# Two bias additions merged into one VectorE operation that reads a shared PSUM product twice

## The chip, the cores and the metric

The kernel runs on one NeuronCore of a Trainium2 chip. The metric is the device time in microseconds of one execution, from launch to the last output byte; the time of a kernel is the median of its runs.

## What is computed

The input `x` is 8 batches of 3136 rows by 256 columns. The reference first mixes each batch in the frequency domain and then applies a gated feed-forward layer:

```python
X = np.fft.rfft(x, axis=1)
Yr = Xr @ w_r - Xi @ w_i + b_r
Yi = Xr @ w_i + Xi @ w_r + b_i
Y  = soft-threshold of (Yr, Yi) by 0.01          # shrink each part towards zero
y  = np.fft.irfft(Y, n=3136, axis=1)
h  = relu(y @ w_in)
g  = sigmoid(depthwise 3-tap convolution of h along the rows)
out = (h * g) @ w_out
```

The two bias vectors `b_r` and `b_i` have one entry per column. They are the data of the change.

## The kernel before, in words

The transform of length 3136 is done as 56 x 56, in two matmul stages each way, with scratch arrays in DRAM between them. The spectral part works in 56 items: 8 batches times 7 groups of 4 frequency columns. Every item passes through these steps, on an order written as one Python loop over `it` in which the steps of different items are interleaved (item `it` in stage 2, item `it-1` in `mix`, item `it-3` in stage 3, and two later pieces of stage 1):

- `stage1` (lines 240 to 248): one matmul of 512 columns per half piece into PSUM (L246), a copy by ScalarE (L247), a store to scratch.
- `stage2` (274 to 290): 16 short matmuls (L281) give the spectrum of an item. ScalarE copies one half to `d` (L284) and rounds the product to the high part `fh` (L285); VectorE makes `d` a difference (L286) and the low part `fl` (L287); then the same for `d` itself: `fh` by ScalarE (L288), `fl` by VectorE (L289). High and low parts exist because the matmuls run on rounded operands, three products for one.
- `mix` (292 to 323): 36 matmuls (L305) into three PSUM tiles `ps[0..2]` (printed as ps_mx), first `ps[2]`, the product that the real and the imaginary result have in common, then `ps[0]` and `ps[1]`. Each `ps[c]` is 128 partitions by 512 fp32 elements, one buffer each. VectorE adds `ps[2]` to the two halves of the bias tile, which gives `p1` (L310, twice; printed as p); adds `p1` to `ps[0]` and `ps[1]`, four additions on 64 partitions each, which gives `v` (L314); ScalarE makes `r = relu(v - 0.01)` (L319); VectorE makes the thresholded `v` (L320); ScalarE rounds it to `sh` (L321); GpSimd makes the rest `sl = v - sh` (L322). `p1`, `r` and `sl` have one buffer, `v` and `sh` two.
- `stage3` (325 to 335): 12 matmuls (L332) on `sh` and `sl`, a copy by ScalarE (L334), a store.

Beside the items, in iterations 3 to 55, a "background" generator converts the 64-bit weights `w_in` and `w_out` to two fp32 parts: eight pieces of 512 elements per partition, each some eleven VectorE operations (L185 to L192, L200, L201) and one ScalarE rounding (L199). Five steps of it are taken per iteration at first, later two or three.

The feed-forward part follows: `stage4` (L424 to L431), `up` (L433 to L459) and `down` (L464 to L485), driven by the loop from L502 on. It holds most of the matmuls (L443 and L471).

The order in which an engine meets its instructions is not the program order alone: a scheduler with a timeline model of its own sorts them per engine when the kernel is built, so a cheaper or dearer operation can move its neighbours. On the chip every engine then runs its list strictly in order. The semaphore waits follow from the tiles.

Of the kernel before, what the change touches and what calls it, by code (L numbers as in the profile page):

```python
# [13 lines left out]
ALU = mybir.AluOpType  # L14
# [3 lines left out]
B, S, D, FF = 8, 3136, 256, 1024  # L18
# [6 lines left out]
UG = 4  # L25
# [70 lines left out]
def spectral_ffn_kernel(ctx: ExitStack, tc: tile.TileContext, x, w_r, w_i, b_r, b_i,  # L96
                        w_in, conv_w, w_out, fwd1, fwd2, inv1, inv2, out):
    nc = tc.nc
    K1, K2 = 2 * R, 2 * SP
# [16 lines left out]
    with ExitStack() as ab:  # L116
# [15 lines left out]
        bias = cmx.tile([P, 2, UG // 2, D], F32, name="bias")  # L132
# [159 lines left out]
        def mix(xs):  # L292


            fh, fl = xs
            ps = [psm.tile([K2, UG // 2, D], F32, name=f"ps_mx{c}") for c in range(3)]
            for c in (2, 0, 1):
                q = (1, 2, 0)[c]
                for k in range(UG // 2):
                    mm = []  # L300
                    for t in range(NT):
                        a = [f[:, t, c, 2 * k:2 * k + 2, :] for f in (fh, fl)]
                        mm += [(a[0], wmix_hi[:, t, q, :]), (a[0], wmix_lo[:, t, q, :]), (a[1], wmix_hi[:, t, q, :])]
                    for n, (lt, rh) in enumerate(mm):
                        nc.tensor.matmul(ps[c][:, k, :], lt, rh, start=(n == 0), stop=(n == len(mm) - 1))  # L305
            p1 = wk.tile([K2, 2, UG // 2, D], F32, name="p1", bufs=1)
            v = wk.tile([K2, UG // 2, 2, D], F32, name="v")
            half = (slice(0, SP), slice(SP, K2))
            for c in range(2):
                nc.vector.tensor_tensor(p1[:, c], ps[2], bias[:, c], op=ALU.add)  # L310
            for c in range(2):
                for k in range(2):
                    src, dst = half[k], half[k if c == 0 else 1 - k]
                    nc.vector.tensor_tensor(v[dst, :, k, :], ps[c][src], p1[src, c], op=ALU.add)  # L314
            v = v.rearrange("p a b d -> p (a b) d")
            sh = wk.tile([K2, UG, D], F32R, name="sh")
            sl = wk.tile([K2, UG, D], F32R, name="sl", bufs=1)
            r = wk.tile([K2, UG, D], F32, name="r", bufs=1)
            nc.scalar.activation(r, v, AF.Relu, bias=mlam)  # L319
            thr = nc.vector.scalar_tensor_tensor(v, v, LAM, r, op0=ALU.add, op1=ALU.min)  # L320
            nc.scalar.copy(sh, v)  # L321
            SL_ENG.tensor_tensor(sl, v, sh.bitcast(F32), op=ALU.subtract)  # L322
            return sh, sl, thr
# [22 lines left out]
        p1 = NG  # L346
# [27 lines left out]
        for it in range(n_it + 3):  # L374
            if it + 2 < n_it:
                a2s[it + 2], _ = load_a2(*items[it + 2])
            if it < n_it:
                xs[it] = stage2(items[it][1], a2s.pop(it))
            if it < NG:
                load_inv1(it)  # L380
                if it + 1 < NG:
                    load_t2(it + 1)
            if 0 <= it - 1 < n_it:
                ss[it - 1] = mix(xs.pop(it - 1))
            if 0 <= it - 3 < n_it:
                stage3(*items[it - 3], ss.pop(it - 3))
            while p1 < n_it and p1 < min(it + AHEAD, NG + 2 + it + it // 2):
                stage1(*items[p1])
                p1 += 1
            if WP0 <= it < n_it:  # L390
                with tc.issue_after(ss[it - 1][2].ins):
                    for _ in range(5 if it < CW_IT else 2 + (it % 5 == 0)):
                        next(background, None)
# [148 lines left out]
```

## Time and profile before

| what | value |
|---|---|
| runs, us | 1767.83, 1800.61, 1798.17; median 1798.17 |
| profiled execution | span 1797.0 us; the page gives no other time for it |
| busy in the span | PE 97%, PE weight load 91%, DVE 87%, ACT 68%, POOL 8% |
| mean granted TensorE clock | 0.993 of full speed |
| spectral part | about 50 to 600 us |
| feed-forward part | about 600 to 1797 us |

The span runs from the first to the last instruction of the profiled execution; the median of the runs is 1.2 us above it. PE is TensorE's matmuls, PEld its weight loads, DVE VectorE, ACT ScalarE, POOL GpSimd. In a row of a timeline the first number is the start in us from the beginning of the span, the second the length; rows of equal operations that follow each other are merged with a count. Recorded lengths of neighbours on one engine overlap by a little, so the distance from one start to the next (the pitch) tells what an instruction really takes away from its engine. DVE "busy" also counts the time in which a started instruction is held up.

### The profile page before, as it was taken

What the parts mean: (1) busy time and instruction counts of PE and PEld (TensorE: products, weight loads), DVE (VectorE), ACT (ScalarE), POOL (GpSimd) and SP (SyncE); (2) the same over time, 40 slices, a digit from 0 to 9 for tenths busy, and PEclk for the clock granted to TensorE, in tenths of its full rate; (3) what the DMA queues carried; (4) which work ended last, traced back from release to release, by engine and by line L of the source; (5) the groups of instructions that cost most, each with busy time, mean ns of one, the idle gap of its engine ahead of it and who ended that gap; (6) DMA issues with size and microseconds to landing.
All of it is one profiled execution on the core that took longest, in us unless ns stands there. A gap on an engine that the chain in (4) does not pass through costs nothing.

```text
span 1797.0 us, 29407 instructions
## 1 busy us (share of the span) xinstructions
PE 1745.9 (97%) x12096; PEld 1627.7 (91%) x12096; DVE 1568.6 (87%) x1842; ACT 1223.6 (68%) x1579; POOL 134.9 (8%) x60
## 2 busy tenths in 40 slices
PE   6999999999999999999999999999999999999999
PEld 2788788888898899999999999999999999999998
DVE  2899999999998698888888898888888888888887
ACT  2666666666666677777677777767777777767766
POOL 0122222222223000000000000000000000000000
PEclk8999999999999999999999999999999999999999
DMA  9776676666562410011111001101101111100001
GB/s 257 224 244 207 177 213 191 186 201 202 164 168 72 132 52 21 22 52 52 32 52 52 32 32 52 52 32 52 52 26 58 52 42 42 42 22 21 21 22 42
DMA packets 107382, 164.63 MB, mean 92 GB/s; under 512 B 8816, under 2 KB 86000, under 8 KB 107248
## 3 DMA queue, kind: packets, MB, share of 16 engines
q1 hardware_dynamic: 107248, 162.74, 30.6%
q8 instruction: 96, 1.57, 0.4%
q14 instruction: 38, 0.31, 0.1%
HBM read 85.65 MB, written 77.07 MB: 91 GB/s over the span
## 4 chain that ended last, share of the span: by engine, by line
PE 70%; DVE 15%; issue 8%; DMA 3%; ACT 3%; SPq 0%; DVEq 0%; ACTq 0%
PE acc L471 31%; PE ps_h L443 31%; PE ps_s L424 5%; DVE v L314 5%; DVE fl L287 2%; PE ps_mx L305 2%; DMA i_raw<-in_inv_dram 2%; DVE p L310 2%; ACT r L319 2%; DVE fl L289 2%; DVE d L286 1%; DVE v L320 1%; PE ps_s L332 1%; PE ps_s L281 1%; DMA z<-sc 0%
## 5 line engine op out<-in xcount | busy, mean ns | idle before, releaser
L471 PE MATMUL acc<-wout,gh 128*128 128x256 f32 x3136 | 567.0, 280 | 0.0
L452 DVE SCALAR_TENSOR_TENSOR c<-h,cw,c 128x896 f32<-128x896 f32 x448 | 512.9, 1147 | 47.1 <-ACT c L450 46.1
L443 PE MATMUL ps_h<-yh,win 128*128 128x450 f32 x1792 | 550.8, 368 | 0.2
L471 PEld LDWEIGHTS acc<-wout,gh 128*128 128x128 f32 x3136 | 493.7, 188 | 6.5
L471 PE MATMUL acc<-wout,gl 128*128 128x256 f32 x1568 | 437.6, 281 | 0.0
L445 ACT ACTIVATE h<-ps_h 128x900 f32<-128x900 f32 x224 | 207.7, 927 | 254.6 <-PE ps_h L443 254.6
L443 PEld LDWEIGHTS ps_h<-yh,win 128*128 128x128 f32 x1792 | 338.7, 189 | 26.3 <-DVE yl L431 0.7
L443 PE MATMUL ps_h<-yl,win 128*128 128x450 f32 x896 | 329.2, 367 | 0.0
L471 PEld LDWEIGHTS acc<-wout,gl 128*128 128x128 f32 x1568 | 293.6, 188 | 0.1
L458 DVE TENSOR_TENSOR gl<-c,gh 128x896 fp32r<-128x896 f32 x224 | 243.1, 1089 | 53.6 <-ACT gh L457 50.1
L454 DVE TENSOR_TENSOR c<-h,c 128x896 f32<-128x896 f32 x224 | 243.5, 1087 | 46.8 <-ACT c L453 46.6
L457 ACT CAST gh<-c 128x896 fp32r<-128x896 f32 x224 | 209.9, 942 | 49.4 <-DVE c L454 49.4
L453 ACT ACTIVATE c<-c 128x896 f32<-128x896 f32 x224 | 213.5, 953 | 23.9 <-DVE c L452 21.0
L305 PE MATMUL ps_mx<-wmix_hi,fl 128*128 128x256 f32 x672 | 193.1, 289 | 17.8 <-DVE fl L289 16.6
L305 PE MATMUL ps_mx<-wmix_hi,fh 128*128 128x256 f32 x672 | 201.2, 300 | 1.1 <-DVE p L310 1.1
L305 PE MATMUL ps_mx<-wmix_lo,fh 128*128 128x256 f32 x672 | 199.9, 298 | 0.0
L443 PEld LDWEIGHTS ps_h<-yl,win 128*128 128x128 f32 x896 | 169.0, 189 | 11.0
L450 ACT ACTIVATE c<-h,cw 128x896 f32<-128x896 f32 x168 | 175.6, 1045 | 2.6 <-DVE gl L458 0.2
L322 POOL TENSOR_TENSOR sl<-v,sh 128x1024 fp32r<-128x1024 f32 x56 | 134.7, 2405 | 451.3 <-PE ps_s L332 240.6
L305 PEld LDWEIGHTS ps_mx<-wmix_hi,fl 128*128 128x128 f32 x672 | 126.0, 188 | 34.0 <-DVE fl L289 25.0
L314 DVE TENSOR_TENSOR v<-ps_mx,p 64x512 f32<-64x512 f32 x224 | 153.8, 687 | 3.3
L305 PEld LDWEIGHTS ps_mx<-wmix_lo,fh 128*128 128x128 f32 x672 | 126.6, 188 | 12.7 <-issue 12.7
(87 smaller groups left out, 2065.9 us busy)
## 6 DMA issues: line engine op xcount, KB each, us to landing
a<-sc SPq DMA_DIRECT2D x56, 448.0 KB, 5.6
sc<-z SPq DMA_DIRECT2D x56, 448.0 KB, 3.4
z<-sc SPq DMA_DIRECT2D x56, 448.0 KB, 3.8
xr<-in_x_dram SPq DMA_DIRECT2D x55, 448.0 KB, 5.2
out_dram<-o SPq DMA_DIRECT2D x27, 896.0 KB, 4.0
sc<-a SPq DMA_DIRECT2D x49, 448.0 KB, 3.9
sc<-ha SPq DMA_DIRECT2D x7, 448.0 KB, 4.8
win_bits<-in_moe_w_in_dram SPq DMA_DIRECT2D x4, 512.0 KB, 5.7
```

What stands on the lines that cost most here:

```text
L305: nc.tensor.matmul(ps[c][:, k, :], lt, rh, start=(n == 0), stop=(n == len(mm) - 1))
L314: nc.vector.tensor_tensor(v[dst, :, k, :], ps[c][src], p1[src, c], op=ALU.add)
L322: SL_ENG.tensor_tensor(sl, v, sh.bitcast(F32), op=ALU.subtract)
L443: nc.tensor.matmul(ps[:, a, 0:CH + 2], lt, rh, start=(n == 0), stop=(n == len(mm) - 1))
L445: nc.scalar.activation(h, ps[:, :, 0:CH + 2], AF.Relu)
L450: nc.scalar.mul(c, h[:, :, 0:CH], cw[:, 0, f:f + 1])
L452: nc.vector.scalar_tensor_tensor(c, h[:, :, k:k + CH], cw[:, k, f:f + 1], c, op0=ALU.mult, op1=ALU.add)
L453: nc.scalar.activation(c, c, AF.Sigmoid)
L454: nc.vector.tensor_tensor(c, h[:, :, 1:CH + 1], c, op=ALU.mult)
L457: nc.scalar.copy(gh, c)
L458: nc.vector.tensor_tensor(gl, c, gh.bitcast(F32), op=ALU.subtract)
L471: nc.tensor.matmul(acc[m // 2][:, m % 2, :], lt[:, sl], rh[:, f, :], start=(f == 0 and n == 0 and m % 2 == 0), stop=(f == NF - 1 and n == ...
```

## The change

The two additions of `ps[2]` and a bias half become one addition over both halves. Its first input is `ps[2]` with a new axis of length 2 and step 0, so it is read twice:

```diff
             p1 = wk.tile([K2, 2, UG // 2, D], F32, name="p1", bufs=1)
             v = wk.tile([K2, UG // 2, 2, D], F32, name="v")
             half = (slice(0, SP), slice(SP, K2))
-            for c in range(2):
-                nc.vector.tensor_tensor(p1[:, c], ps[2], bias[:, c], op=ALU.add)
+            nc.vector.tensor_tensor(p1, ps[2].unsqueeze(1).broadcast_to([K2, 2, UG // 2, D]), bias, op=ALU.add)
             for c in range(2):
                 for k in range(2):
```

56 pairs of 512-element additions become 56 additions of 1024 elements. Lines behind it are one lower in the changed kernel: L310 becomes L309, L314 becomes L313, L319 and L320 become L318 and L319. The scheduler moves a few other instructions. SP's list differs by one swap of two loads at the start, GpSimd's list is the same, PE's list differs in the interleaving of some stage 1 and stage 3 matmuls with the mix matmuls, above all at the start and where the background work ends.

VectorE in the 22nd and 23rd item, where a piece of `w_in` is being converted (p is `p1`, ps_mx one of the three products, win_rest and win_m parts of the weight conversion). Before:

```order
L310 TENSOR_TENSOR p_2664<-ps_mx_2627,bias 128x512 x2
L320 SCALAR_TENSOR_TENSOR v<-v,r 128x1024
L191 TENSOR_SCALAR win_r<-win_bits 128x512
L289 TENSOR_TENSOR fl<-d,fh 128x2x256
L314 TENSOR_TENSOR v<-ps_mx_2625,p_2664 64x2x256 x2
L314 TENSOR_TENSOR v<-ps_mx_2626,p_2664 64x2x256 x2
L192 SCALAR_TENSOR_TENSOR win_rest<-win_r,win_e 128x512
L286 TENSOR_TENSOR d<-ps_s_2713,d 128x256
```

The same place after the change:

```order
L309 TENSOR_TENSOR p_2643<-ps_mx_2606,bias 128x1024
L319 SCALAR_TENSOR_TENSOR v<-v,r 128x1024
L191 TENSOR_SCALAR win_r<-win_bits 128x512
L289 TENSOR_TENSOR fl<-d,fh 128x2x256
L313 TENSOR_TENSOR v<-ps_mx_2604,p_2643 64x2x256 x2
L192 SCALAR_TENSOR_TENSOR win_rest<-win_r,win_e 128x512
L313 TENSOR_TENSOR v<-ps_mx_2605,p_2643 64x2x256 x2
L286 TENSOR_TENSOR d<-ps_s_2691,d 128x256
```

The two additions are one, and the weight operation L192, which stood behind the four additions to `v`, now stands between them. This move occurs in five of the eight weight pieces.

ScalarE one item later (s is the product of stage 2, a the output of stage 1). Before:

```order
L284 COPY d<-ps_s_2825 128x256
L285 CAST fh<-ps_s_2825 128x512
L284 COPY d<-ps_s_2834 128x256
L319 ACTIVATE r<-v,small 128x1024
L285 CAST fh<-ps_s_2834 128x512
L247 COPY a_2805<-ps_s_2809 112x512
L321 CAST sh<-v 128x1024
```

After the change:

```order
L284 COPY d<-ps_s_2802 128x256
L285 CAST fh<-ps_s_2802 128x512
L318 ACTIVATE r<-v,small 128x1024
L284 COPY d<-ps_s_2811 128x256
L285 CAST fh<-ps_s_2811 128x512
L247 COPY a_2782<-ps_s_2786 112x512
L320 CAST sh<-v 128x1024
```

The second copy to `d` of the next item, which stood ahead of `r`, now stands behind it.

## Prediction

> **What bounds the kernel now.** I read the page's head and its chain, then the stretches of time, then who waits for whom, then the rows of VectorE beside those of GpSimd.
>
> ```profile
> span 1797.0 us, 29407 instructions
> PE 1745.9 (97%) x12096; PEld 1627.7 (91%) x12096; DVE 1568.6 (87%) x1842; ACT 1223.6 (68%) x1579; POOL 134.9 (8%) x60
> PE 70%; DVE 15%; issue 8%; DMA 3%; ACT 3%; SPq 0%; DVEq 0%; ACTq 0%
> ```
>
> The busy time of each engine in the stretches (columns: stretch, length, then busy us and count for PE, PEld, DVE, ACT, POOL):
>
> ```profile
> 50.00:160.00 110.00, 105.58 (x757) 91.37 (x756) 100.32 (x175) 72.62 (x119) 26.40 (x11) 1.00 0.75 225
> 160.00:506.00 346.00, 329.07 (x2381) 287.58 (x2380) 338.30 (x490) 220.02 (x356) 81.50 (x35) 1.00 0.65 191
> 506.00:577.00 71.00, 66.89 (x556) 65.16 (x554) 70.05 (x115) 47.66 (x69) 22.05 (x9) 1.00 0.46 126
> 600.00:1797.00 1197.00, 1192.51 (x8168) 1147.63 (x8166) 1035.36 (x1027) 857.20 (x999) 0.00 (x0) 1.00 0.13 40
> ```
>
> The last row is two thirds of the span, TensorE is busy in nearly all of it, and no bias addition of a mix runs there. In the three rows above, VectorE is busy 91%, 98% and 99% of the time, so at first sight it is the bound of the spectral part, and the change would pay in full. The waits say otherwise (columns: total us, times, longest). First PE and PEld from 160 to 506, then both from 506 to 577:
>
> ```profile
> PE ps_mx L305 <- DVE fl L289: 14.9, 22, 1.2
> ```
> ```profile
> PEld ps_mx L305 <- DVE fl L289: 21.7, 29, 1.4
> ```
> ```profile
> PE ps_mx L305 <- DVE fl L289: 1.7, 2, 1.2
> ```
> ```profile
> PEld ps_mx L305 <- DVE fl L289: 2.4, 3, 1.4
> ```
>
> TensorE waits for VectorE some 15 to 22 us out of 346, nearly always for `fl` of L289, and 2 us out of 71 later. The rest of the time it has matmuls to do. So everything that a faster VectorE could ever bring here is about 24 us (21.7 + 2.4), and what has to become faster is L289. What does L289 wait for? VectorE's own rows:
>
> ```profile
> 250.51 1.41 DVE L190 TENSOR_TENSOR win_m<-win_m,win_e 128x512 int32<-128x512 int32 x1
> ...
> 257.15 1.28 DVE L310 TENSOR_TENSOR p<-ps_mx,bias 128x512 f32<-128x512 f32 x2
> 258.35 1.22 DVE L320 SCALAR_TENSOR_TENSOR v<-v,r 128x1024 f32<-128x1024 f32 x1
> 259.48 0.42 DVE L191 TENSOR_SCALAR win_r<-win_bits 128x512 int32<-128x512 int32 x1
> 259.81 0.68 DVE L289 TENSOR_TENSOR fl<-d,fh 128x512 fp32r<-128x512 f32 x1
> ...
> 263.26 0.69 DVE L192 SCALAR_TENSOR_TENSOR win_rest<-win_r,win_e 128x512 f32<-128x512 int32 x1
> 263.96 0.42 DVE L286 TENSOR_TENSOR d<-ps_s,d 128x256 f32<-128x256 f32 x1
> ...
> 264.90 1.22 DVE L320 SCALAR_TENSOR_TENSOR v<-v,r 128x1024 f32<-128x1024 f32 x1
> ...
> 267.57 1.28 DVE L310 TENSOR_TENSOR p<-ps_mx,bias 128x512 f32<-128x512 f32 x2
> 268.76 2.67 DVE L201 TENSOR_TENSOR win<-win_m,win_rest 128x512 fp32r<-128x512 f32 x1
> ...
> 278.40 1.28 DVE L310 TENSOR_TENSOR p<-ps_mx,bias 128x512 f32<-128x512 f32 x2
> 279.60 1.99 DVE L289 TENSOR_TENSOR fl<-d,fh 128x512 fp32r<-128x512 f32 x1
> ...
> 289.14 1.75 DVE L187 TENSOR_SCALAR win_e<-win_e 128x512 int32<-128x512 int32 x1
> ```
>
> and GpSimd's in the same time:
>
> ```profile
> 268.53 2.36 POOL L322 TENSOR_TENSOR sl<-v,sh 128x1024 fp32r<-128x1024 f32 x1 [5.31 <-PE ps_s L332]
> 278.68 2.36 POOL L322 TENSOR_TENSOR sl<-v,sh 128x1024 fp32r<-128x1024 f32 x1 [7.78 <-PE ps_s L332]
> ...
> 317.66 2.36 POOL L322 TENSOR_TENSOR sl<-v,sh 128x1024 fp32r<-128x1024 f32 x1 [5.31 <-PE ps_s L332]
> ```
>
> The same L289 takes 0.68 us at 259.81 and 1.99 at 279.60. GpSimd's `sl` ends at 278.68 + 2.36 = 281.04, L289 at 279.60 + 1.99 = 281.59, which is 0.55 later; L201 at 268.76 ends 0.54 after the `sl` of 268.53. So these VectorE instructions stand still until `sl` is over and then take their half microsecond. The 98% hold such standing time. And `sl` itself waits for the stage 3 matmuls (L332) that free its one buffer. That is a ring: matmuls, `sl`, a held VectorE instruction, `fl`, matmuls. The bias additions stand in front of the held instruction, in its shadow.
>
> **The change part by part.** It removes 112 additions and adds 56. Their price, by row (mean ns of one in the second number behind the bar):
>
> ```profile
> L458 DVE TENSOR_TENSOR gl<-c,gh 128x896 fp32r<-128x896 f32 x224 | 243.1, 1089 | 53.6 <-ACT gh L457 50.1
> L310 DVE TENSOR_TENSOR p<-ps_mx,bias 128x512 f32<-128x512 f32 x112 | 71.7, 681 | 0.1
> L320 DVE SCALAR_TENSOR_TENSOR v<-v,r 128x1024 f32<-128x1024 f32 x56 | 70.5, 1258 | 11.1 <-ACT r L319 11.1
> L431 DVE TENSOR_TENSOR yl<-ps_s,yh 128x896 fp32r<-128x896 f32 x56 | 64.3, 1151 | 15.7 <-ACT yh L430 13.4 <-issue 2.1
> ```
>
> Two additions last 2 x 681 = 1362 ns as records, but neighbours overlap: the pair at 278.40 is followed at 279.60, so it takes 1.20 us of the engine; the pair at 257.15, followed at 258.35, the same. The merged one has 1024 elements; L320, with as many, is followed after 1.13 us (258.35 to 259.48). I take 1.14 and a saving of **0.06 us per mix**, 56 x 0.06 = 3.4 us of VectorE time. No row shows an operation that reads a PSUM tile twice, so I bound it. Above, scaling the record of L458 gives 1089 x 1024 / 896 = 1245 ns, a saving of 1362 - 1245 = 117 ns, 6.6 us for 56. Below, L431, which reads PSUM and has the dearest rate per element, gives 1151 x 1024 / 896 = 1315 ns, or some 1.23 us when the same 0.08 of overlap goes off: 0.03 us worse than the pair, 1.7 us lost for 56. The merged operation is nearest to L310 itself (same operands, straight rows), where only the fixed part of one instruction goes away, so I stay with 0.06.
>
> [...]
>
> How much of 0.06 per mix lies on the path? The additions run in three stretches:
>
> ```profile
> 50.00:160.00 110.00, 15.46 (x24) 1.00 0.75 225
> 160.00:506.00 346.00, 44.76 (x70) 1.00 0.65 191
> 506.00:577.00 71.00, 11.52 (x18) 1.00 0.46 126
> ```
>
> That is 12, 35 and 9 mixes. From 506 on, TensorE waits for VectorE 2.4 us in all, so the 9 mixes bring nothing: what hides them is the matmuls of mix and stage 3. From 160 to 506, 29 of 35 items show a wait of the weight loads for L289. The pattern repeats every five items (the `sl` of 317.66 has the same wait as that of 268.53, 49.13 us earlier), as the background work does, and in four of these five an instruction behind the additions is held by `sl`: L190 at 250.51, L201, L289 and L187 above. What p gives back, that instruction stands longer. One item in five (257.15 to 259.81) has nothing held, and there L289 comes 0.06 earlier: 7 x 0.06 = 0.4 us. Before 160 I count nothing either, since TensorE is occupied (105.58 of 110). If all of this cover were gone, the price would be the 3.4 us.
>
> **The moved instructions.** In five weight pieces L192 now precedes two of the four additions to `v`, so `r` starts 0.70 us later (263.26 to 263.96). ScalarE there:
>
> ```profile
> 263.26 1.15 ACT L319 ACTIVATE r<-v,small 128x1024 f32<-128x1024 f32 x1 [0.40 <-DVE v L314]
> 266.20 1.06 ACT L321 CAST sh<-v 128x1024 fp32r<-128x1024 f32 x1 [0.56 <-DVE v L320]
> ```
>
> `r` would end at 263.96 + 1.15 = 265.11 instead of 264.41; L320, at 264.90 now, would start at about 265.15, a quarter of a microsecond later, and `sh` would end at 267.5 instead of 267.26. `sl` starts at 268.53 because of L332, so a full microsecond is left: cost nothing; without that slack it is 0.70 at worst. The other move puts one copy to `d` behind `r`:
>
> ```profile
> 272.88 0.39 ACT L284 COPY d<-ps_s 128x256 f32<-128x256 f32 x1
> 274.80 1.16 ACT L319 ACTIVATE r<-v,small 128x1024 f32<-128x1024 f32 x1 [1.54 <-DVE v L314]
> 275.86 0.56 ACT L285 CAST fh<-ps_s 128x512 fp32r<-128x512 f32 x1
> 277.31 1.05 ACT L321 CAST sh<-v 128x1024 fp32r<-128x1024 f32 x1 [0.39 <-DVE v L320]
> ```
>
> The copy goes from an idle 1.54 us into a place behind `r`, and shifts L285 and L247 by about 0.26; `sh` has 0.39 of idle time ahead of it, so this is nothing too. The matmuls of stage 1 and 3 that change places are the same matmuls on a full engine: nothing.
>
> **Sum.** 1797.0 - 0.4 = 1796.6 us for the span, and 1.2 us for what lies between the span and the median of the runs (1798.17): **1797.8 us**, no change.
>
> **The rivals.**
>
> *VectorE is the bound after all.* For it: 98% busy, and 15% of the chain. Against it: the small waits of TensorE. Then all 56 mixes pay, 3.4 us by pitch or 6.6 by records: 1798.2 - 3.4 = 1794.8 down to 1791.6.
>
> *Slower: the delayed threshold.* The place is L192 in front of the additions to `v`; price up to 0.70 us in each of five pieces, 3.5 us, from the point at which `sh` ends later than the stage 3 matmuls that free `sl`. Since `sl` holds VectorE, the delay would pass to L289 and to the matmuls. With the double read at its dear bound (1.7 us) on top of no gain, it ends at 1798.2 + 3.5 + 1.7 = 1803.4. Against it: one microsecond of slack.
>
> *The ring falls into another rhythm.* If the held instructions no longer met `sl`, TensorE's waits could go, all 24 us of them: 1774. L201 misses the start of `sl` by only 268.76 - 268.53 = 0.23 us, which speaks for it; but when it goes first, L289 behind it meets the same `sl`. One of the three runs shown, 1767.83, lies 30.3 us under the median, and no row of this profile says why; a median of the changed kernel may fall near it, at 1767, without the change having done anything. I count both together.
>
> *The merge does not take place.* The row 128x1024 in the instruction list leaves no room for that; I give it nothing.
>
> **How the numbers follow.** Forecast 0.68, VectorE bound 0.08, slower 0.08, another rhythm or a low median 0.16. For the range I go from 1764, which holds the low run less the 3.4 us, to 1804, just above the slower rival. Two per cent, 36 us, is about what a measurement of this kernel can tell from no change. No rival reaches it by its own price; only a gain on top of a low median does (0.03), or something on the slower side that I have not seen (0.02); 0.95 remains for within 2%.
>
> **What would show it.** Right: the row of the merged addition has count 56 and near 1.2 us, its distance to the next start is about 1.14; L289 and L201 still end about half a microsecond behind `sl`, having stood longer; TensorE's waits for L289 stay at 15 to 22 us from 160 to 506; the spectral part keeps its length within 1 us. Wrong: a merged operation of 1.3 us or more; `sl` waiting for `sh` rather than L332 where L192 has moved; a spectral part shorter by 3 us or more while TensorE's clock is the same, which would say that VectorE's own time was the path; or a change in the feed-forward part, for which nothing here has a cause.

## The result and the profile after

| kernel | runs, us |
|---|---|
| before, four runs beside the change | 1767.63, 1767.83, 1798.17, 1800.61 |
| changed, four runs | 1791.85, 1793.09, 1793.34, 1795.64; median 1793.21 |

The kernel before has two times here, about 1768 and about 1799. So it goes in 75 of 78 more runs beside the experiments: 41 lie from 1765.96 to 1775.90 and 34 from 1794.62 to 1802.50. Three lie far above (1902.62, 2508.41 and 7617.22 us, with a granted clock of 0.846, 0.636 and 1.0 in their records), which nothing here explains. The changed kernel has one time. Ratios, here and below, are to the runs of the kernel before in its lower group, and runs more than 1.5% above a kernel's fastest are left out of them. The ratio is 1.013, with an interval from 1.0116 to 1.0143: 1.3% slower. To the execution whose profile the prediction was made from (span 1797.0) it is a little faster. Both are true, and the reason is the same.

The head of the page after, and the merged addition and the moved weight operation by line:

```profile
span 1793.6 us, 29287 instructions
PE 1742.9 (97%) x12096; PEld 1625.7 (91%) x12096; DVE 1562.8 (87%) x1786; ACT 1223.2 (68%) x1579; POOL 133.8 (7%) x60
```
```profile
L309 DVE TENSOR_TENSOR p<-ps_mx,bias 128x1024 f32<-128x1024 f32 x56 | 68.2, 1217 | 0.1
L192 DVE SCALAR_TENSOR_TENSOR win_rest<-win_r,win_e 128x512 f32<-128x512 int32 x4 | 6.7, 1667 | 0.1
```

The merged addition lasts 1217 ns and is what was forecast. L192 is not: 1667 ns on average, where the row of 263.26 in the kernel before had 0.69 us. Now GpSimd's `sl` after the change:

```profile
196.78 2.36 POOL L321 TENSOR_TENSOR sl<-v,sh 128x1024 fp32r<-128x1024 f32 x1 [6.76 <-PE ps_s L331]
205.91 2.36 POOL L321 TENSOR_TENSOR sl<-v,sh 128x1024 fp32r<-128x1024 f32 x1 [6.77 <-PE ps_s L331]
215.04 2.40 POOL L321 TENSOR_TENSOR sl<-v,sh 128x1024 fp32r<-128x1024 f32 x1 [6.78 <-PE ps_s L331]
224.66 2.36 POOL L321 TENSOR_TENSOR sl<-v,sh 128x1024 fp32r<-128x1024 f32 x1 [7.21 <-PE ps_s L331]
234.22 2.36 POOL L321 TENSOR_TENSOR sl<-v,sh 128x1024 fp32r<-128x1024 f32 x1 [7.21 <-PE ps_s L331]
244.13 2.36 POOL L321 TENSOR_TENSOR sl<-v,sh 128x1024 fp32r<-128x1024 f32 x1 [7.55 <-PE ps_s L331]
255.88 2.38 POOL L321 TENSOR_TENSOR sl<-v,sh 128x1024 fp32r<-128x1024 f32 x1 [9.39 <-ACT sh L320]
```

Up to 215.04 the starts are 9.13 us apart. From there they are 9.6 to 11.8 us apart, the pattern that the prediction took for the kernel's own. What happens on VectorE just before:

```profile
203.97 0.69 DVE L289 TENSOR_TENSOR fl<-d,fh 128x512 fp32r<-128x512 f32 x1
204.57 2.10 DVE L313 TENSOR_TENSOR v<-ps_mx,p 64x512 f32<-64x512 f32 x3
206.69 2.13 DVE L192 SCALAR_TENSOR_TENSOR win_rest<-win_r,win_e 128x512 f32<-128x512 int32 x1
208.83 0.69 DVE L313 TENSOR_TENSOR v<-ps_mx,p 64x512 f32<-64x512 f32 x1
...
213.42 1.22 DVE L309 TENSOR_TENSOR p<-ps_mx,bias 128x1024 f32<-128x1024 f32 x1
214.55 0.68 DVE L201 TENSOR_TENSOR win<-win_m,win_rest 128x512 fp32r<-128x512 f32 x1
215.15 2.85 DVE L289 TENSOR_TENSOR fl<-d,fh 128x512 fp32r<-128x512 f32 x1
```

L192, in its new place, meets the `sl` of 205.91 and stands until it is over (208.27): 2.13 us instead of 0.69. The last addition to `v` waits behind it, `r` and all that follows is late, and one item on L289 comes at 215.15, just 0.11 us after the next `sl` began at 215.04. It is held, lasts 2.85 us, and from then on VectorE always comes too late.

### The profile page after: what moved, and what is told of

The parts are those of the page before. It is cut to its first block, busy times and chain, and to the rows that moved or that the text cites. A ratio compares the mean times of both kernels' runs of the same rounds, so it can differ in the third digit from the quotient of the medians.

```text
span 1793.6 us, 29287 instructions
## 1 busy us (share of the span) xinstructions
PE 1742.9 (97%) x12096; PEld 1625.7 (91%) x12096; DVE 1562.8 (87%) x1786; ACT 1223.2 (68%) x1579; POOL 133.8 (7%) x60
## 4 chain that ended last, share of the span: by engine, by line
PE 75%; DVE 13%; issue 6%; ACT 2%; DMA 2%; SPq 0%; DVEq 0%; ACTq 0%
PE acc L470 31%; PE ps_h L442 31%; PE ps_s L423 5%; DVE v L313 4%; PE ps_mx L305 4%; DVE p L309 2%; ACT r L318 2%; DVE fl L287 2%; DVE fl L289 2%; PE ps_s L246 2%; PE ps_s L331 1%; PE ps_s L281 1%; DMA i_raw<-in_inv_dram 1%; DVE d L286 1%; DMA z<-sc 0%
## 5 line engine op out<-in xcount | busy, mean ns | idle before, releaser
L313 DVE TENSOR_TENSOR v<-ps_mx,p 64x512 f32<-64x512 f32 x224 | 153.9, 687 | 3.2
```

## The experiments

Theory A: the spectral part has **two rhythms**. In the quick one L289 runs ahead of `sl`, no matmul waits for it, and an item takes 9.13 us. In the slow one an instruction behind the bias additions meets `sl`, L289 comes late, the matmuls wait, the next `sl` waits for those, and an item takes about 9.8 us. The new order of the lists pushes the ring into the slow one. Theory B: the merged operation itself is dear. Theory C: something outside the program makes the two times of the kernel before.

To separate the operation from the order, the instruction lists were fixed by ordering edges between neighbours (order only, no waits), with the lists read from a build of the one or the other kernel:

```diff
+def keep_order(tc):
...
+        for a, b in zip(seq, seq[1:]):
+            tc.add_manual_dep(b, a.name, mybir.DependencyInfo(
+                mybir.DependencyClass.NoSync, mybir.DependencyReason.DATA), reason="issue_after")
...
             accs = down(ci, f, gs.pop(st - LAG), accs)
+    keep_order(tc)
```

Line numbers in these kernels are higher by the lines added: L192 is L207 there, L289 is L304, `sl` L336 or L337, the weight loads of a mix L320.

**E1, two additions, old lists (a control).**

> The kernel before with every engine's list of instructions fixed to the list that it had: a control. Theory A (two rhythms): the spectral part runs in one of two rhythms of the ring matmuls - sl - held VectorE instruction - fl; about 9.13 us per item or about 9.82. The kernel before falls into the slow one in some executions, by a near miss of L289 against sl at about 158.8 us, and stays in the quick one in others: runs near 1767 and runs near 1799, nothing between; in a profile of a run near 1767 the starts of sl stay 9.13 us apart from 160 to about 500 us. Theory C (something outside the program, such as the chip's own state): in a run near 1767 the starts of sl have the same pattern as in a run near 1799, and all parts are shorter.

12 runs: six from 1767.26 to 1770.86, six from 1795.85 to 1801.32. This time the profile is of a quick run (span 1766.7). GpSimd's `sl`, and what the weight loads wait for from 160 to 500 us:

```profile
195.10 2.37 POOL L337 TENSOR_TENSOR sl<-v,sh 128x1024 fp32r<-128x1024 f32 x1 [6.76 <-PE ps_s L347]
204.23 2.37 POOL L337 TENSOR_TENSOR sl<-v,sh 128x1024 fp32r<-128x1024 f32 x1 [6.76 <-PE ps_s L347]
213.39 2.36 POOL L337 TENSOR_TENSOR sl<-v,sh 128x1024 fp32r<-128x1024 f32 x1 [6.80 <-PE ps_s L347]
222.53 2.36 POOL L337 TENSOR_TENSOR sl<-v,sh 128x1024 fp32r<-128x1024 f32 x1 [6.77 <-PE ps_s L347]
```
```profile
PEld ps_mx L320 <- issue: 17.1, 69, 0.3
PEld ps_s L296 <- PE ps_s L347: 8.7, 34, 0.3
PEld ps_s L296 <- issue: 8.2, 34, 0.2
PEld ps_mx L320 <- PE ps_mx L320: 0.3, 1, 0.3
```

9.13 to 9.16 us from start to start, and the wait for L289, 21.7 us in the profile of the kernel before, is gone from the list. With the same lists, then, this kernel runs in either rhythm. The place where the two part is the item at 158 us. VectorE and GpSimd in the profile of the kernel before, then in that of E1:

```profile
157.62 1.28 DVE L310 TENSOR_TENSOR p<-ps_mx,bias 128x512 f32<-128x512 f32 x2
158.81 2.74 DVE L289 TENSOR_TENSOR fl<-d,fh 128x512 fp32r<-128x512 f32 x1
```
```profile
158.66 2.35 POOL L322 TENSOR_TENSOR sl<-v,sh 128x1024 fp32r<-128x1024 f32 x1 [6.80 <-PE ps_s L332]
```
```profile
156.73 1.28 DVE L325 TENSOR_TENSOR p<-ps_mx,bias 128x512 f32<-128x512 f32 x2
157.93 0.68 DVE L304 TENSOR_TENSOR fl<-d,fh 128x512 fp32r<-128x512 f32 x1
```
```profile
158.56 2.36 POOL L337 TENSOR_TENSOR sl<-v,sh 128x1024 fp32r<-128x1024 f32 x1 [6.81 <-PE ps_s L347]
```

L289 comes 0.15 us behind `sl` in the one, 0.63 us ahead of it in the other. Theory C falls as far as the pattern goes. The 0.8 us by which VectorE is late come from a hold of the same kind, at 102 us. VectorE is then at nearly the same point in both executions, but `sl` starts at 100.94 in the slow one and at 102.37 in the quick one. So L188 of a small weight piece, which stands between the additions to `v`, meets `sl` in the slow one only; it is L203 in E1, the second line:

```profile
102.27 1.08 DVE L188 SCALAR_TENSOR_TENSOR cw_e<-cw_bits,cw_e 128x8 int32<-128x8 int32 x1
```
```profile
102.18 0.17 DVE L203 SCALAR_TENSOR_TENSOR cw_e<-cw_bits,cw_e 128x8 int32<-128x8 int32 x1
```

L289 at 112.47 is then held too (1.97 us, against 0.69 at 111.48 in E1). Why `sl` starts 1.43 us apart there stays open; the two executions differ from their first `sl` on, at 63.67 and 62.37 us.

**E2, the merged addition, old lists.**

> The merged addition, with every engine's list kept as it was before the change. Theory A with the order as the cause (the weight operation L192 between the additions to v is held by sl and throws the ring into the slow rhythm): with the old order the ring stays in the quick rhythm, 1765 to 1768 us in nearly all runs; the merged addition is 0.06 us quicker, so L289 at 158.8 us wins more often against sl than before. Theory B (the merged operation itself, its length or its double read, makes the kernel slower): 1790 to 1796 us as the changed kernel.

12 runs, 1766.26 to 1772.34; ratio 1.0003 (0.9993 to 1.0012). Theory B falls: the merged operation costs nothing, and every run is quick.

**E3, two additions, new lists.**

> The two additions, with every engine's list as the scheduler made it for the merged one. Theory A with the order as the cause: slow rhythm in every run, 1793 to 1801 us. Theory B: as the kernel before, runs near 1767 and near 1799.

Six runs, 1795.91 to 1803.95; ratio 1.0175 (1.0161 to 1.0189). With the new lists two additions are slow in every run, where E1 had six quick runs of 12. The moved L192 is not what this profile shows, though. It loses the quick rhythm 50 us before the first L192 between additions (at 209.63), where the kernel before loses it, with L289 0.15 us behind `sl`:

```profile
156.81 2.75 DVE L304 TENSOR_TENSOR fl<-d,fh 128x512 fp32r<-128x512 f32 x1
```
```profile
156.66 2.35 POOL L337 TENSOR_TENSOR sl<-v,sh 128x1024 fp32r<-128x1024 f32 x1 [6.80 <-PE ps_s L347]
```

What the place of L192 does is shown by E4 and E5.

**E4, the changed kernel with its own lists, L192 put behind the additions to `v`** (in the six pieces where the change had put it between; the sections above count five, since one of them stood between the third and the fourth).

> The changed kernel with its own lists, except that in the six weight pieces where L192 stands between the additions to v it is put right behind them. Theory A with L192 as the one cause: quick rhythm, 1765 to 1769 us in nearly all runs. Theory A with another move as the cause (the copy to d behind r, the stage 1 and stage 3 matmuls): 1790 to 1796 as the changed kernel. Theory B: 1790 to 1796.

12 runs, 1767.0 to 1772.74; ratio 1.0008 (0.9998 to 1.0018). Of all the moves in the lists, this one makes the changed kernel slow.

**E5, the reverse: the merged addition with the old lists, only L192 moved between the additions.** In VectorE's list, at each of the six pieces:

```diff
 v<-ps_mx,p
 v<-ps_mx,p
+win_rest<-win_r,win_e
 v<-ps_mx,p
 v<-ps_mx,p
-win_rest<-win_r,win_e
```

> The merged addition with the old lists (quick rhythm in all its runs, 1766 to 1772), and one move only: the weight operation L192 stands between the second and the third addition to v in all six pieces where the change had put it there. If L192 in that place is enough by itself: slow rhythm in every run, 1790 to 1797. If it needs the other moves of the changed lists too: 1766 to 1774.

Four runs, 1791.01 to 1794.42; ratio 1.0139 (1.0119 to 1.0159). Enough by itself.

**E6, only the first of the six moved; E7, only the fourth.** The edit is that of E5, in one piece.

> As the run with all six moved, but only the first of the six (at about 205 us). If both rhythms sustain themselves, one push is enough and the rest of the background stretch stays slow: some 30 items at 0.69 us more, 1788 to 1796, with sl 9.8 us apart from there on. If every L192 only costs its own hold: about 1.4 us and back to the quick rhythm, 1768 to 1773.

> As before, but only the fourth of the six (at about 340 us). If one push is enough: quick until then, slow for the some 16 items behind it, 16 x 0.69 = 11 us, about 1780. If L192 only costs its own hold: 1768 to 1773.

E6: four runs, 1788.95 to 1796.79, median 1793.35, ratio 1.014 (1.011 to 1.0171). E7: four runs, 1779.18 to 1784.07, median 1782.53, ratio 1.0078 (1.0056 to 1.01). One push is as dear as six, and about half as dear when it comes half way. In E7 the `sl` on either side of the push, and VectorE at it:

```profile
324.50 2.36 POOL L336 TENSOR_TENSOR sl<-v,sh 128x1024 fp32r<-128x1024 f32 x1 [6.77 <-PE ps_s L346]
333.63 2.37 POOL L336 TENSOR_TENSOR sl<-v,sh 128x1024 fp32r<-128x1024 f32 x1 [6.77 <-PE ps_s L346]
342.76 2.36 POOL L336 TENSOR_TENSOR sl<-v,sh 128x1024 fp32r<-128x1024 f32 x1 [6.76 <-PE ps_s L346]
351.92 2.35 POOL L336 TENSOR_TENSOR sl<-v,sh 128x1024 fp32r<-128x1024 f32 x1 [6.80 <-PE ps_s L346]
362.05 2.36 POOL L336 TENSOR_TENSOR sl<-v,sh 128x1024 fp32r<-128x1024 f32 x1 [7.77 <-PE ps_s L346]
371.62 2.36 POOL L336 TENSOR_TENSOR sl<-v,sh 128x1024 fp32r<-128x1024 f32 x1 [7.21 <-PE ps_s L346]
```
```profile
342.85 2.82 DVE L207 SCALAR_TENSOR_TENSOR wout_rest<-wout_r,wout_e 128x512 f32<-128x512 int32 x1
345.68 1.39 DVE L328 TENSOR_TENSOR v<-ps_mx,p 64x512 f32<-64x512 f32 x2
...
352.10 2.73 DVE L216 TENSOR_TENSOR wout<-wout_m,wout_rest 128x512 fp32r<-128x512 f32 x1
354.75 0.68 DVE L304 TENSOR_TENSOR fl<-d,fh 128x512 fp32r<-128x512 f32 x1
```

9.13 us apart before, held at 342.85 for 2.82 us, held again one item later at 352.10, and 10.1, 9.6 from there on, with no further L192 out of place. The ring does not find back by itself while the background work lasts.

**E8, the changed kernel with its own lists, in which GpSimd writes zeros instead of the difference** (the low part of stage 3's input is left out):

```diff
-            SL_ENG.tensor_tensor(sl, v, sh.bitcast(F32), op=ALU.subtract)
+            SL_ENG.memset(sl.bitcast(F32), 0.0)
```

> The changed kernel with its own lists; GpSimd writes zeros to sl instead of v - sh (leaves out the low part of the inverse transform's input), so that it reads nothing and is done sooner. If the hold of VectorE instructions by sl is what makes the new place of L192 dear: L192 between the additions takes its 0.69 us again, and the ring stays in the quick rhythm, 1764 to 1770. If the new order is slow for another reason (r late, matmuls late): 1788 to 1796 still.

Four runs, 1763.49 to 1769.32, median 1763.95; ratio 0.9982 (0.9956 to 1.0009). L192 is between the additions, and takes its time again:

```profile
L207 DVE SCALAR_TENSOR_TENSOR win_rest<-win_r,win_e 128x512 f32<-128x512 int32 x4 | 2.8, 690 | 0.1
```

So it is the hold by `sl` that makes the place dear. The GpSimd instruction was also shorter here (951 ns) and needs neither `v` nor `sh`, so this run does not tell apart whether the shorter time or the absence of a read ends the hold.

**E9 and E10, the saving given back.** In E2 not one of 12 runs fell into the slow rhythm, in E1 six of 12. The lists are the same, so the merged addition's 0.06 us per mix should be what lets L289 win. To test it, a small instruction was put behind each merged addition, a write of one element in E9, an addition of eight elements that reads the same PSUM tile in E10:

```diff
             nc.vector.tensor_tensor(p1, ps[2].unsqueeze(1).broadcast_to([K2, 2, UG // 2, D]), bias, op=ALU.add)
+            nc.vector.memset(small[:, 16:17], 0.0)
```
```diff
+            nc.vector.tensor_tensor(small[:, 16:24], ps[2][:, 0, 0:8], small[:, 24:32], op=ALU.add)
```

> The merged addition with the old lists, and behind every merged addition one more VectorE instruction, a write of one element per partition to an unused column, so that the saving of about 0.06 us per mix is given back (a little more than given back: such small instructions follow each other after 0.08 us). If the merged addition is quick in all 12 runs because these 0.06 us let L289 win its race against sl at about 158 us, the runs split again as with two additions: some near 1768, some near 1798. If the quick runs have another cause (one instruction less to be held, the double read), all runs stay at 1766 to 1774.

> As the run with the one-element write, whose extra instruction ran beside its neighbour and cost nothing; now the extra instruction behind every merged addition is a real addition of 8 elements that reads the same PSUM tile (as short additions of that size in the kernel before are followed after 0.08 us). If the merged addition is quick in all runs because its shorter time keeps L289 ahead of sl, the runs split again: some near 1768, some near 1798, and in a slow one L289 at about 158 us starts just behind sl. If not, all 12 stay at 1766 to 1774, and why two additions flip and one doesn't stays open.

E9: 12 runs, 1766.59 to 1772.89. But it tested nothing, since the write cost nothing:

```profile
136.07 1.22 DVE L324 TENSOR_TENSOR p<-ps_mx,bias 128x1024 f32<-128x1024 f32 x1
137.21 0.42 DVE L301 TENSOR_TENSOR d<-ps_s,d 128x256 f32<-128x256 f32 x1
137.24 0.06 DVE L325 MEMSET small<- 128x1 f32 x1
```

The next instruction starts 1.14 us after the merged addition, as without the write. It stands behind the write in VectorE's list, yet its recorded start lies 0.03 us ahead of the write's, so the starts do not follow the list strictly there. In E10 the small addition does take its place:

```profile
135.64 1.22 DVE L324 TENSOR_TENSOR p<-ps_mx,bias 128x1024 f32<-128x1024 f32 x1
136.78 0.15 DVE L325 TENSOR_TENSOR small<-ps_mx,small 128x8 f32<-128x8 f32 x1
136.85 0.41 DVE L301 TENSOR_TENSOR d<-ps_s,d 128x256 f32<-128x256 f32 x1
```

1.21 us to the next start, as long as the pair of additions. Nine of 12 runs lie from 1766.96 to 1771.54, three at 1795.57, 1798.37 and 1798.43: split again. The merged kernels without that time given back (E2, E4, E9, E11) have no such run among 48. No profile shows one of the three, so its L289 was not seen behind `sl`. But the race stands in the other profiles. In the six in which L188 is held at 100 to 104 us, as in the kernel before, two additions bring L289 0.15 us behind the `sl` of 157 to 160 us (the kernel before, E3), and the merged addition brings it 0.18 to 0.20 us ahead (the changed kernel, E4, E7, E11). The changed kernel there:

```profile
160.06 0.68 DVE L289 TENSOR_TENSOR fl<-d,fh 128x512 fp32r<-128x512 f32 x1
```
```profile
160.24 2.73 POOL L321 TENSOR_TENSOR sl<-v,sh 128x1024 fp32r<-128x1024 f32 x1 [6.81 <-PE ps_s L331]
```

In the profiles in which L188 is not held, L289 leads by 0.63 us with two additions (E1), by 0.80 to 0.84 with the merged one (E2, E5, E6, E9), and by 0.61 in E10, whose small addition gives the lead back. So the merge's few hundredths of a microsecond per mix decide the race.

**E11, a version without fixed lists.** The changed kernel with one ordering edge for each L192 from the second weight piece on, which puts it behind the last addition to `v`; the scheduler does the rest. (`late` holds the L192 in question; the lines that fill it are left out here.)

```diff
-                    nc.vector.tensor_tensor(v[dst, :, k, :], ps[c][src], p1[src, c], op=ALU.add)
+                    add = nc.vector.tensor_tensor(v[dst, :, k, :], ps[c][src], p1[src, c], op=ALU.add)
+            for i in late:
+                tc.add_manual_dep(i.ins, add.ins.name, mybir.DependencyInfo(
+                    mybir.DependencyClass.NoSync, mybir.DependencyReason.DATA), reason="issue_after")
+            late.clear()
```

> No fixed lists: the changed kernel, in which one ordering edge per weight piece (from the second on) tells the scheduler to put L192 behind the last addition to v; the scheduler sorts the rest itself, and its lists differ from both kernels. If L192 in the shadow of sl is the one thing that throws the ring out of its rhythm: 1765 to 1773 in all runs. If the quick rhythm depends on the old lists as such: runs at 1785 or more.

12 runs, 1766.29 to 1772.63, median 1771.26; ratio 1.0011 (0.9999 to 1.0022). It is as fast as the kernel before at its best, in all 12 runs. It beats the changed kernel by some 22 us, and the kernel before on the average of its two rhythms.

## Why the prediction was wrong, by its own steps

- **The moved instructions: wrong, and the step that failed.** The prediction gave L192 what it took in its old place, 0.70 us of delay with a microsecond of slack behind, and so a cost of nothing. It had just read that L289 and L201 stand still while `sl` runs (1.99 us at 279.60, 2.67 at 268.76), and did not ask whether the new place lies under `sl`. Its own profile has the answer, an `sl` from 260.83 to 263.22, over the place behind the second of the four additions (260.42 to 263.23):

```profile
260.83 2.39 POOL L322 TENSOR_TENSOR sl<-v,sh 128x1024 fp32r<-128x1024 f32 x1 [9.46 <-ACT sh L321]
```

The moved L192 is held in both rhythms. In the slow one it takes 1.93 us (at 256.88 after the change), and the five items from one such piece to the next take 49.43 us, against 49.13 before: 0.3 us per piece. In the quick one it takes 2.13 us after the change and 2.82 in E6 and E7, and that one push costs some 0.7 us in every item behind it, 23 us in all (E6 against E2). Behind the additions a hold costs little (E1's own L207 at that place is held as well, 1.27 us at 205.87, in the quick rhythm); between them it delays `v`, `r` and the next item's L289.
- **What bounds the kernel: right for the profiled execution, and wrong as a picture of the kernel.** The ring of matmuls, `sl`, a held instruction and `fl` is there. But the five-item pattern is only one of two rhythms, and the profile was of the slow one. In the quick one TensorE has no wait for L289 at all (E1, 160 to 490 us). The waits that the prediction read as a ceiling for any gain, "about 24 us", are most of the distance between the two: the last `sl` starts at 554.47 us in the quick execution of E1 and at 584.0 in that of the kernel before.
- **The sum.** Against the execution it was made for, 1797.0, it said 0.4 us less; the changed kernel's span is 3.4 us shorter, 1793.6, and for another reason than the one given: it keeps the quick rhythm until 215 us, while that execution had lost it at 158. Most of the signs named for "right" came true (count 56, 1217 ns, 1.13 us to the next start, 19.1 us of waits of the weight loads for L289), since this profile too is mostly of the slow rhythm. Two signs named for "wrong" came as well: behind the moved L192 the `sl` of 263.94 waits for `sh`, where that of 268.53 waited for L332, and the last `sl` starts at 579.23 instead of 584.0, here because the quick rhythm lasts longer.
- **The price of the merged addition: right; what it is worth: wrong.** 1.14 us to the next start was taken, 1.13 to 1.14 is measured. (Of the rows used as bounds L310 itself, not L431, has the dearest time per element, 681 / 512 = 1.33 ns; nothing came of it.) In the slow rhythm the saving is hidden as forecast: five items take 49.11 us with the merged addition and L192 in its old place (E6, 265.60 to 314.71), 49.13 before. But "Before 160 I count nothing either" left out the place where it decides the rhythm, L289 against `sl` at about 158 us (E10). "What hides them" from 506 on is wrong by a little: the items there come 7.57 us apart (529.40, 536.98, 544.55) where they came 7.64 apart, so VectorE does bind those, 0.07 us each, half a microsecond in all.
- **The rivals.** "The ring falls into another rhythm" named the mechanism, but as a way for the change to gain, by L201 escaping `sl`, and it counted the low run of 1767.83 beside it without taking the one for a sign of the other. By its time that run was the kernel before in the quick rhythm; the changed kernel loses that rhythm in every run. "Slower: the delayed threshold" had the right instruction at the right place and priced it as a sum of five delays of up to 0.70 us; in the slow rhythm the delays are there, 0.3 us each, but what made the kernel slow is one push, after which each item costs 0.7 us more (E6, E7). "VectorE is the bound after all" fell: E2 is level with the quick runs of E1.
- **Within 2%** held: 1.3%.

Which instructions `sl` holds is read from the rows alone. L192 and L289, with two inputs in SBUF, are held (2.13 us at 206.69 and 2.85 at 215.15 after the change); in E8, where GpSimd only writes zeros, they average 690 and 685 ns. The additions to `v`, with one input in PSUM, are not: all 224 of them in the profile of the kernel before last 673 to 696 ns, and four in the quick execution of E1 take 2.81 us, 0.70 each, although the `sl` of 204.23 runs over the second half:

```profile
203.03 2.81 DVE L329 TENSOR_TENSOR v<-ps_mx,p 64x512 f32<-64x512 f32 x4
```

And where L289 comes first, `sl` is the longer one (2.73 us at 160.24 us after the change, with L289 at 160.06, against 2.36 at 169.38). Two inputs in SBUF are not the only case: L187, with one, is held as well (1.75 us at 289.14 before the change, 0.42 at 186.29 after it). What makes an instruction one that is held was not shown, since no run varies its inputs alone.

## What to carry to other kernels

When a change moves instructions, price each move in its new place: what runs on the other engines at that time, and whether the moved instruction can be held by it. Where a group of runs lies a few per cent apart from the others, compare the spacing of one repeated instruction over the whole stretch before any sum is made, since the loop through several engines had two steady rhythms here (9.13 us and about 9.8 us per item), and one late instruction decided between them (E6, E7). An ordering edge that keeps such instructions out of the way (E11) was worth some 22 us here, against the 3.4 us of VectorE time that the merge saves.

## What was not expected of the hardware

- The VectorE addition that reads a 512-element PSUM tile twice through an axis of step 0 was no slower than an operation that reads its inputs once: 1217 ns for 1024 elements after the change, against 1224 ns in the median of L320 with as many before it (1258 on average, rows held by `sl` among them).
- A one-element write by VectorE ran within the time of the instruction beside it (E9, 0.06 us at 137.24, within the 0.42 us of L301 from 137.21): with 56 of them per execution the median was 1769.10 us, against 1769.93 in E2.
- A ring through four engines stayed in the rhythm into which it was pushed for 29 items (E6, 216.51 to 503.95 us), and changed over within two.
